# Broadcast products on VectorE, and late zero fills from SBUF, in a decode block's backward pass

## The chip, the cores and the metric

The kernel runs on one core of one Trainium2 chip. The metric is the device time of one execution in microseconds; the time before is the median of three runs. A separate view of one of these executions, the profile, records every instruction of the core's engines (PE = TensorE, DVE = VectorE, ACT = ScalarE, POOL = GpSimd, SP = SyncE) and every packet of its 16 DMA engines. L307 stands for line 307 of the kernel before, unless the kernel after is named.

## What is computed

One token passes an attention block with a sliding window over a long cache, then a gated MLP; the reference returns the output and the gradients of everything it was given.

```python
W = 4096                                   # of Sk = 32768 cached positions; 16 heads share 8 K/V heads, Dh = 256
q = layernorm(x) @ wq
p = softmax(q . k_cache[:, :, Sk-W:] / 16)
h = x + (p @ v_cache[:, :, Sk-W:]) @ wo    # D = 448
n = layernorm(h)
h2 = h + ((n @ w_gate) * (n @ w_up)) @ w_down   # F = 1792
out, vjp = jax.vjp(f, x, k_cache, v_cache, wq, wo, w_gate, w_up, w_down)
return out, *vjp(grad_out)
```

The gradients of both caches have the caches' full shape, 8 x 32768 x 256 in bf16 (134 MB each), and only the last 4096 positions of each head are not zero. So out_2 (dk) and out_3 (dv) are 235 MB of zeros and 34 MB of computed rows; the other gradients are 12 MB. The inputs that must be read are some 54 MB.

## The kernel before

**Memory.** Nearly everything lives in one tile, `arena`, [128, TOTAL] bf16, cut by hand into regions: `zeros` = columns 0 to 8191 (16 KB per partition); six 16 KB buffers A_off[0..5] behind it, which hold V of most heads and later serve as staging; M_sb (moments, f32); and a region RB reused by every stage. Columns 8192 to 16383 are A_off[0].

**Zero fills.** `fills` is a list of 103 regions of 2 MB. POOL issues them on its own queue (q0) straight from `zeros`: 42 with the full 16 KB row per partition (L135), then 13 that read only the first half of `zeros` twice (L133, packets of 8 KB), because the second half is soon needed as the weight buffer of MLP block 1. After block 1 is done, that half is zeroed again (L429) and POOL issues the remaining 48 (L430, L135). The last 18.9 MB of zeros, in head 7, are the `late_jobs`: four regions of 4 MB and one of 2 MB, issued by SP at the end of the source (L662 to L681).

**First pass** (L265 to L339). For each of 8 heads: K and V loaded by SP (L199), K transposed on PE (L255), scores, softmax, and moments, whose products are one DVE tensor_tensor of 128x2048 with a broadcast f32 operand (L307). Then wo in two halves (L322).

**Middle** (L356 to L479). Output projection (L377), layernorm, and the MLP in three blocks of 640, 512 and 640 columns. Block n's gate and down weights come through SP (L352 to L354), the up weights through ACT's queue. Blocks 0 and 2 share one buffer (in RB), block 1 uses the second half of `zeros`: its load must wait until the 42 full-width fills have read it. Per block: products with the weights (L406), diagonal expansions, and the weight-gradient reductions (L424). Then the gradients through layernorm and wo.

**Second pass** (L491 to L654). Heads in the order 2 to 7, 0, 1. For each: V transposed and dotted, a small [128, 128] factor rT, and R_sb, [128, 512], the right-hand side common to all rows. `Rbig`, [128, 8, 512], holds R_sb multiplied by each of eight masks tl_f[:, l] (L632, eight tensor_scalars per head); 32 matmuls take slices of it (L639), and their results are cast by DVE and ACT (L643 to L647) into the staging of dv (in place of V) and dk (two buffers in turn). SP stores both (L649). A staging buffer of dk is free again when the store of two heads earlier has landed.

Between heads, jobs build the weight gradients in two staging buffers `wst` (A_off[3] and A_off[4], in turn): `job_o` the rows of dwo, dh_bc times a column of oX_f, 16 tensor_scalars of 448 columns for each half; `job_d` those of dw_down, 14 of them; `job_q` and `job_qB` dwq; `expand_dg` and `job_g` dw_gate and dw_up (stores L578, L579). All use the helper scale_into (L534). At the end of the seventh head's turn DVE zeroes columns 8192 to 16383 (L654), once the store that reads them has landed.

**What sets the order.** The program text is reordered for each engine by the framework's scheduler, which keeps dependences; each engine then runs its list in order, and a DMA waits in its issuer's list. That is why SP's copies of L681, last in the source, stand among the K loads of the first pass: their source is zeros already written to DRAM, so they depend on early fills alone. The order that matters here is the one of the built programs. SP's list before, from the second pass on, is: stores of heads one to three, both parts of dwo, head four, dw_down, head five, dw_down's last part, dwq, the 2 MB late fill, dwq's last part, head six, dw_gate and dw_up, head seven, head eight.

Of the kernel before, what the change touches and what calls it, by code (L numbers as in the profile page):

```python
# [7 lines left out]
bf16 = mybir.dt.bfloat16  # L8
f32 = mybir.dt.float32
AX = mybir.AxisListType.X  # L10
ALU = mybir.AluOpType
ACT = mybir.ActivationFunctionType

D = 448
# [4 lines left out]
W = 4096  # L19
T = 32  # L20
F = 1792
NF = 14
BLOCKS = [(0, 5), (640, 4), (1152, 5)]
Sk = 32768
EPS = 1e-5
SCALE = 1.0 / 16.0
ZW = 8192
# [6 lines left out]
def kernel(  # L34
        ctx, tc, A_x, A_k_cache, A_v_cache, A_wq, A_wo, B_x, B_w_gate, B_w_up, B_w_down, grad_out,
           out_0, out_1, out_2, out_3, out_4, out_5, out_6, out_7, out_8):
    nc = tc.nc
    LD = nc.sync
# [14 lines left out]
    def ar(off, n):  # L53
        return arena[:, off:off + n]
# [4 lines left out]
    zeros = ar(0, ZW)  # L59
# [36 lines left out]
    dh2_bc = const.tile([128, D], bf16)  # L96
# [13 lines left out]
    nc.vector.memset(ones_f[:], 1.0)  # L110
    eps_t = const.tile([128, 1], f32)
    nc.vector.memset(eps_t[:], EPS)

    scratch = nc.dram_tensor("zero_row", [4 * ZW], bf16, kind="Internal").ap()
    LD.dma_start(out=scratch.rearrange("(p f) -> p f", f=ZW // 32), in_=zeros[:, 0:ZW // 32])

    def zero_rows(o, g, n0, n1, f):
        reg = o[0, g, 0:Sk - W, :].rearrange("s d -> (s d)")[n0 * 128 * ZW:n1 * 128 * ZW]
# [4 lines left out]
    for g in range(G):  # L123
        for o in (out_2, out_3):
            if g == G - 1 and o is out_3:
                continue
            reg = zero_rows(o, g, 0, 5 if g == G - 1 else NZ, ZW)
# [25 lines left out]
    tl_f = const.tile([128, 8], f32)  # L153
# [205 lines left out]
    with tc.tile_pool(name="ps_mid", bufs=3, space=bass.MemoryType.PSUM) as ps_mid, \  # L359
# [11 lines left out]
        oX_f = const.tile([128, 32], f32)  # L371
# [17 lines left out]
        hh_f = const.tile([128, NF], f32)  # L389
# [4 lines left out]
        for n in range(len(BLOCKS)):  # L394
            f0, nb, w, wgu, wd = block_views(n)
            b0 = f0 // 128
            cs = slice(b0, b0 + nb)
            for b in range(nb):
                nc.vector.tensor_tensor_reduce(out=dgb[:, 0:D], in0=wd[:, b, :], in1=dh2_bc[:], scale=1.0, scalar=0.0,
                                               op0=ALU.mult, op1=ALU.add, accum_out=d_hh[:, b0 + b:b0 + b + 1])  # L400
# [11 lines left out]
            for i in range(2):  # L412
                nc.vector.tensor_tensor(out=diag[:, 0:w].rearrange("p (m b) -> p m b", b=nb), in0=ident_f[:].unsqueeze(2).to_broadcast([128, 128, nb]),
                                        in1=dgu_f[:, i, cs].unsqueeze(1).to_broadcast([128, 128, nb]), op=ALU.mult)
# [6 lines left out]
            for c in range(4):  # L421
# [3 lines left out]
                                               op0=ALU.mult, op1=ALU.add, accum_out=dhn[0:kp, c, n:n + 1])  # L425
# [9 lines left out]
        dh_bc = const.tile([128, D], bf16)  # L435
# [18 lines left out]
        for jc in range(32):  # L454
            nc.vector.tensor_tensor_reduce(out=wo_sb[:, jc, :], in0=wo_sb[:, jc, :], in1=dh_bc[:], scale=1.0, scalar=0.0,  # L455
                                           op0=ALU.mult, op1=ALU.add, accum_out=doX_f[:, jc:jc + 1])
# [3 lines left out]
                                in1=m8_f[:].unsqueeze(2).to_broadcast([128, 8, 32]), op=ALU.mult)  # L460
# [13 lines left out]
        for dh in range(2):  # L474
# [11 lines left out]
                                scalar1=SCALE, scalar2=None, op0=ALU.mult)  # L486
# [4 lines left out]
    with tc.tile_pool(name="work2", bufs=2) as work2, tc.tile_pool(name="lnw", bufs=1) as lnw, \  # L491
# [17 lines left out]
        for c in range(3):  # L509
            nc.vector.tensor_tensor_reduce(out=wq2A[:, c, :], in0=wq2A[:, c, :], in1=dq_bc, scale=1.0, scalar=0.0,  # L510
                                           op0=ALU.mult, op1=ALU.add, accum_out=dn1[:, c:c + 1])
# [22 lines left out]
        def scale_into(out, src, col):  # L534
            nc.vector.tensor_scalar(out=out, in0=src, scalar1=col, scalar2=None, op0=ALU.mult)  # L535

        def job_o(n):
            def run():
                buf = buffer()
                for j in range(16):  # L540
                    scale_into(buf[:, j * D:(j + 1) * D], dh_bc[:], oX_f[:, 16 * n + j:16 * n + j + 1])
                LD.dma_start(out=out_5.rearrange("(p j) n -> p (j n)", j=32)[:, 16 * n * D:16 * (n + 1) * D], in_=buf[:, 0:16 * D])
            return run

        def job_d():
            buf = buffer()
            for j in range(NF):
                scale_into(buf[:, j * D:(j + 1) * D], dh2_bc[:], hh_f[:, j:j + 1])
            for f0, nb in BLOCKS:
                b0 = f0 // 128  # L550
                LD.dma_start(out=out_8[f0:f0 + 128 * nb, :].rearrange("(p b) n -> p (b n)", b=nb), in_=buf[:, b0 * D:(b0 + nb) * D])
# [49 lines left out]
        for it, g in enumerate(order):  # L601
            V_sb = kv_at(V2_off[it])
            fill_vpad(it % 2, doT_bf[:, :, 2 * g:2 * g + 2])

            def evac(q, XT, ps):
                if q % 2:
                    nc.scalar.copy(out=XT, in_=ps)  # L607
                else:
                    nc.vector.tensor_copy(out=XT, in_=ps)  # L609
            dpT_ps = dots(V_sb, VT_slot, vpad[it % 2], rows2, ps_t, "tmp", evac)  # L610

            pds = work2.tile([128, 4, 8, 4], bf16, tag="pds")
            pv = pT_all[:, g].rearrange("p (q l) h -> p q l h", q=4)
            tmp = work2.tile([128, T, 2], f32, tag="tmp2")
            nc.vector.tensor_tensor(out=tmp[:], in0=dpT_ps[:].rearrange("p q l h -> p (q l) h"),
                                    in1=delta_bc[:, 2 * g:2 * g + 2].unsqueeze(1).to_broadcast([128, T, 2]), op=ALU.subtract)
            nc.vector.tensor_copy(out=pds[:, :, :, 0:2], in_=pv)
            nc.vector.tensor_tensor(out=pds[:, :, :, 2:4], in0=tmp[:].rearrange("p (q l) h -> p q l h", q=4), in1=pv, op=ALU.mult)
            r_ps = ps_t.tile([128, 128], bf16, tag="tmp")
            nc.tensor.transpose(r_ps[:], pds[:].rearrange("p q l i -> p (q l i)"), ident_bf[:])  # L620
            rT = work2.tile([128, 128], bf16, tag="rT")
            nc.vector.tensor_copy(out=rT[:], in_=r_ps[:])
            nc.vector.tensor_copy(out=Zr, in_=Z4[:, :, :, g, :].rearrange("p w e i -> p (w e) i").unsqueeze(2).to_broadcast([128, 4, 32, 4]))
            R_ps = ps_t.tile([128, 2, 2, 128], f32, tag="tmp")
            for w in range(2):
                for dh in range(2):
                    nc.tensor.matmul(R_ps[:, w, dh, :], lhsT=Zr[:, 2 * w + dh].rearrange("p k i -> p (k i)"), rhs=ident_bf[:], start=True, stop=True)
            R_sb = work2.tile([128, 512], bf16, tag="R", bufs=1)
            nc.scalar.copy(out=R_sb[:], in_=R_ps[:].rearrange("p w e n -> p (w e n)"))
            RB_ = Rbig[it % 2]  # L630
            for l in range(8):
                nc.vector.tensor_scalar(out=RB_[:, l, :], in0=R_sb[:], scalar1=tl_f[:, l:l + 1], scalar2=None, op0=ALU.mult)  # L632
            stV, stK = V_sb, kv_at(dK_off[it % 2])
            for l in range(8):
                for qp in range(2):
                    d_ps = ps_d.tile([128, 2, 2, Dh], f32, tag="d")
                    for qi in range(2):
                        q = 2 * qp + qi
                        nc.tensor.matmul(d_ps[:, qi].rearrange("p w d -> p (w d)"), lhsT=rT[32 * q:32 * (q + 1), :], rhs=RB_[32 * q:32 * (q + 1), l, :],  # L639
                                         start=True, stop=True)  # L640
                    t = 4 * l + 2 * qp
                    if qp:
                        nc.scalar.copy(out=stV[:, t:t + 2, :], in_=d_ps[:, :, 0, :])  # L643
                        nc.scalar.copy(out=stK[:, t:t + 2, :], in_=d_ps[:, :, 1, :])  # L644
                    else:
                        nc.vector.tensor_copy(out=stV[:, t:t + 2, :], in_=d_ps[:, :, 0, :])  # L646
                        nc.vector.tensor_copy(out=stK[:, t:t + 2, :], in_=d_ps[:, :, 1, :])  # L647
            for o_ap, st_ in ((out_3, stV), (out_2, stK)):
                LD.dma_start(out=o_ap[0, g, Sk - W:, :].rearrange("(p t) d -> p t d", t=T), in_=st_)  # L649
            for job in plan[it]:  # L650
                job()
            if it == 6:

                nc.vector.memset(ar(ZW, ZW), 0.0)  # L654

        R64 = 4 * ZW
        done = out_2[0, 0, 0:Sk - W, :].rearrange("s d -> (s d)")
        other = out_3[0, 0, 0:Sk - W, :].rearrange("s d -> (s d)")

        srcs = ["same", "rows16", "rows64", "shift", "other", "scratch", "rows16_32", "same"]  # L660
        n = 0
        for o, g, n0, n1, f in late_jobs:  # L662
            reg = zero_rows(o, g, n0, n1, f)
            for i in range(reg.shape[0]):
                if f == ZW:
                    LD.dma_start(out=reg[i], in_=ar(ZW, f))
                    continue
                flat = reg[i].rearrange("p f -> (p f)")
                kind = srcs[n]
                n += 1  # L670
                w = R64 // 2 if kind == "rows16_32" else R64
                dst = flat.rearrange("(a r b) -> a r b", a=16, b=w)
                m = 2 * 128 * ZW // (16 * w)
                if kind in ("same", "scratch"):
                    src = (scratch if kind == "scratch" else done[0:w]).unsqueeze(0).unsqueeze(0).to_broadcast([16, m, w])
                elif kind in ("rows16", "rows16_32"):
                    src = done[0:16 * w].rearrange("(a r b) -> a r b", a=16, b=w).to_broadcast([16, m, w])
                else:
                    lo = {"rows64": 0, "shift": 5 * 4096 + 3 * R64, "other": 0}[kind]
                    src = (other if kind == "other" else done)[lo:lo + 16 * m * w].rearrange("(a r b) -> a r b", a=16, b=w)  # L680
                LD.dma_start(out=dst, in_=src)  # L681

# [1 line left out]
_INS = ['A_x', 'A_k_cache', 'A_v_cache', 'A_wq', 'A_wo', 'B_x', 'B_w_gate', 'B_w_up', 'B_w_down', 'grad_out']  # L684
# [26 lines left out]
```

## Time and profile before

| | |
|---|---|
| median of 3 runs | 806.97 us (805.34, 807.64, 806.97) |
| the profiled execution | 805.34 us, span 803.6 us |
| PE busy | 464.4 us, 58% |
| DVE busy | 408.8 us, 51% |
| ACT busy | 196.1 us, 24% |
| DMA moved | 334.86 MB |
| first pass ends (last L316) | 314.7 us |
| first computed store of the second pass | 522.0 us |
| last store issued by SP | 751.8 us |
| end of q0's zero fills (landed) | 785.5 us |

The profiled time contains 1.7 us around the span. "Waits" name what ended an engine's idle time. A window's row gives each engine's busy time with its number of instructions, then the granted TensorE clock, the busy share of the DMA engines and what they moved in GB/s. In a timeline row, the bracket is the idle time just before it and what ended that.

### The profile page before, as it was taken

How to read it: one execution, taken by the hardware profiler on the slowest of the kernel's cores; microseconds unless marked ns; L12 is line 12 of the kernel's file. 1: busy time of each engine (PE TensorE's matmuls, PEld its weight loads, DVE VectorE, ACT ScalarE, POOL GpSimd, SP SyncE). 2: the span in 40 equal slices, each digit the busy share in tenths (PEclk: the TensorE clock that was granted, in tenths of full speed). 3: DMA queues.
4: the chain of work that ended last, by engine and by line, in shares of the span. 5: the costliest groups of instructions: out<-in, count | busy, mean ns of one | idle time of the engine just before them, and what ended most of it. 6: DMA issues, size and time to landing. Idle time of an engine off the chain costs nothing.

```text
span 803.6 us, 7904 instructions
## 1 busy us (share of the span) xinstructions
PE 464.4 (58%) x3159; PEld 240.0 (30%) x3182; DVE 408.8 (51%) x728; ACT 196.1 (24%) x309; POOL 61.3 (8%) x112
## 2 busy tenths in 40 slices
PE   0258999999999999241232584958442700744100
PEld 0234545445455454021121471433120300311000
DVE  2115764836748575021378528848666703877200
ACT  0043124132241301000010120736342400645200
POOL 4000000000001010011011000100000000000000
PEclk9998999999999999555555695978665765767555
DMA  9999999999999999999999999999999999999995
GB/s 351 428 432 431 429 430 446 387 432 370 417 422 429 426 426 430 422 426 421 421 427 431 409 425 422 430 429 427 426 429 424 423 425 423 423 419 422 423 426 230
DMA packets 29242, 334.86 MB, mean 417 GB/s; under 512 B 2835, under 2 KB 6038, under 8 KB 7958
## 3 DMA queue, kind: packets, MB, share of 16 engines
q0 software_dynamic: 16496, 216.01, 63.7%
q1 hardware_dynamic: 11270, 116.74, 35.0%
q10 hardware_dynamic: 1440, 1.61, 0.6%
q8 instruction: 25, 0.41, 0.2%
q14 instruction: 11, 0.09, 0.0%
HBM read 70.47 MB, written 280.66 MB: 437 GB/s over the span
## 4 chain that ended last, share of the span: by engine, by line
DMA 41%; another core or an unknown queue 24%; DVE 13%; PE 9%; issue 2%; POOL 2%; ACT 1%; SPq 0%; DVEq 0%; ACTq 0%; POOLq 0%
DMA out_dram<-arena 41%; DVE arena L646 2%; DVE arena L455 2%; DVE arena L647 2%; PE dqb_ps L498 2%; PE rows_ps L258 2%; POOL out_dram L135 2%; DVE arena L510 1%; PE d_ps L639 1%; PE tr_ps L255 1%; DVE arena L535 1%; DVE arena L424 1%; PE dqb_ps L501 1%; DVE arena L632 1%
## 5 line engine op out<-in xcount | busy, mean ns | idle before, releaser
L307 DVE TENSOR_TENSOR arena<-arena,p_f 128x2048 bf16<-128x2048 bf16 x64 | 145.2, 2284 | 59.5 <-PE M_ps L312 59.5
L312 PE MATMUL M_ps<-arena 128*128 128x512 bf16 x489 | 126.4, 381 | 1.1
L255 PE MATMUL tr_ps<-ident_bf,arena 128*128 128x128 bf16 x1024 | 87.6, 236 | 22.4 <-DMA arena<-in_A_k_cache_dram 15.1
L258 PE MATMUL rows_ps<-arena,vpad 128*16 128x512 bf16 x256 | 85.4, 429 | 22.3 <-DVE arena L609 17.1
L135 POOL DMA_DIRECT2D out_dram<-arena x90 | 48.1, 536 | 608.7 <-DMA out_dram<-arena 575.9
L255 PEld LDWEIGHTS <-arena 128*128 128x128 bf16 x1024 | 65.8, 105 | 71.8 <-issue 55.6
L639 PE MATMUL d_ps<-arena,rT 32*128 32x512 bf16 x256 | 43.1, 503 | 64.5 <-DVE arena L647 44.5
L272 ACT COPY arena<-tr_ps 128x1024 bf16<-128x1024 bf16 x64 | 61.8, 1015 | 75.6 <-PE tr_ps L255 75.6
L316 PE MATMUL ok_ps<-arena 128*16 128x256 bf16 x512 | 64.5, 273 | 1.1 <-DVE arena L299 0.9
L312 PEld LDWEIGHTS <-arena 128*128 128x128 bf16 x512 | 43.3, 99 | 50.9 <-issue 15.2
L607 ACT COPY arena<-tr_ps 128x1024 bf16<-128x1024 bf16 x32 | 32.5, 1017 | 97.0 <-PE tr_ps L255 39.6
L643 ACT CAST arena<-d_ps 128x512 bf16<-128x512 f32 x64 | 37.7, 588 | 65.3 <-PE d_ps L639 65.3
L316 PEld LDWEIGHTS <-arena 128*16 128x16 bf16 x512 | 41.9, 89 | 29.8 <-issue 20.8
L646 DVE CAST arena<-d_ps 128x512 bf16<-128x512 f32 x64 | 43.9, 686 | 13.6 <-PE d_ps L639 13.3
L647 DVE CAST arena<-d_ps 128x512 bf16<-128x512 f32 x64 | 43.5, 679 | 8.7 <-DMA out_dram<-arena 8.7
L644 ACT CAST arena<-d_ps 128x512 bf16<-128x512 f32 x64 | 38.2, 596 | 9.3 <-DMA out_dram<-arena 9.3
L639 PEld LDWEIGHTS <-rT 32*128 32x128 bf16 x256 | 11.2, 95 | 90.2 <-issue 51.8
L258 PEld LDWEIGHTS <-vpad 128*16 128x16 bf16 x256 | 18.9, 90 | 56.1 <-issue 48.1
L406 PE MATMUL gu_ps<-X_b,arena 128*128 128x1 bf16 x112 | 10.0, 187 | 28.9 <-DMA arena<-in_B_w_gate_dram 28.8
L287 ACT ACTIVATE e_f<-cols_ps,nbias 128x32 f32<-128x32 f32 x16 | 4.5, 285 | 85.7 <-DVE nbias L283 85.7
L260 DVE COPY arena<-rows_ps 16x512 f32<-16x512 f32 x16 | 10.8, 676 | 28.3 <-PE rows_ps L258 28.3
L510 DVE CUSTOM_DVE_ANT_0 arena<-arena 128x4096 bf16<-128x4096 bf16 x3 | 13.1, 4423 | 23.5 <-ACT arena L503 23.5
(198 smaller groups left out, 381.6 us busy)
## 6 DMA issues: line engine op xcount, KB each, us to landing
out_dram<-arena POOLq DMA_DIRECT2D x103, 2048.0 KB, 54.9
out_dram<-arena SPq DMA_DIRECT2D x18, 2048.0 KB, 29.6
arena<-in_A_v_cache_dram SPq DMA_DIRECT2D x10, 2048.0 KB, 52.0
arena<-in_A_k_cache_dram SPq DMA_DIRECT2D x8, 2048.0 KB, 33.3
arena<-in_A_wq_dram SPq DMA_DIRECT2D x2, 3072.0 KB, 20.6
arena<-in_A_wo_dram SPq DMA_DIRECT2D x2, 1792.0 KB, 18.6
out_dram<-arena SPq DMA_DIRECT2D x2, 1792.0 KB, 33.1
out_dram<-arena SPq DMA_DIRECT2D x2, 1344.0 KB, 48.5
```

The source lines that it names most:

```text
L135: ZQ.dma_start(out=reg, in_=zeros)
L255: nc.tensor.transpose(tr_ps[:, dh, i, :], X_sb[:, 4 * q + i, dh * 128:(dh + 1) * 128], ident_bf[:])
L258: nc.tensor.matmul(rows_ps[:], lhsT=pad[:, dh, 16 * q:16 * q + 16], rhs=XT[:, dh].rearrange("p t k -> p (t k)"), start=(q == 0 and dh == 0 ...
L272: sT_ps = dots(kv_at(K_off[g]), KT_slot, vpad[g % 2], rows1, ps_c, "cols", lambda q, XT, ps: nc.scalar.copy(out=XT, in_=ps))
L307: nc.vector.tensor_tensor(out=pK, in0=K_sb[:, 4 * c:4 * c + 4, :].unsqueeze(2).to_broadcast([128, 4, 2, Dh]), in1=p_f[:, c::8, :].unsqueez ...
L312: nc.tensor.matmul(M_ps[:, vh, :], lhsT=V_sb[:, t, vh * 128:(vh + 1) * 128], rhs=pK[:, i, :, :].rearrange("p h d -> p (h d)"), start=(t == ...
L316: nc.tensor.matmul(ok_ps[:, k, :], lhsT=ppad[g % 2][:, 8 * (t % 4) + t // 4, :], rhs=X_sb[:, t, :], start=(g == 0 and k == 0 and t == 0), ...
L639: nc.tensor.matmul(d_ps[:, qi].rearrange("p w d -> p (w d)"), lhsT=rT[32 * q:32 * (q + 1), :], rhs=RB_[32 * q:32 * (q + 1), l, :], start=T ...
L643: nc.scalar.copy(out=stV[:, t:t + 2, :], in_=d_ps[:, :, 0, :])
L644: nc.scalar.copy(out=stK[:, t:t + 2, :], in_=d_ps[:, :, 1, :])
L646: nc.vector.tensor_copy(out=stV[:, t:t + 2, :], in_=d_ps[:, :, 0, :])
L647: nc.vector.tensor_copy(out=stK[:, t:t + 2, :], in_=d_ps[:, :, 1, :])
```

## The change

Three edits of the computing code and one of the fills:

1. The eight masked copies of R_sb per head become one tensor_tensor of 128x4096, R_sb broadcast over the masks times tl_f broadcast over the columns (f32).
2. Each half of dwo's rows becomes one tensor_tensor of 128x7168 and
3. dw_down's rows one of 128x6272, in the same manner.
4. The four late 4 MB regions are no longer copied from zeroed DRAM in several patterns of source, but stored from columns 0 to 16383 of `arena`, 32 KB per partition, after both halves are zero; the 2 MB one is stored from columns 8192 to 16383 as before. The 64 KB DRAM scratch row and its store are gone.

```diff
-    scratch = nc.dram_tensor("zero_row", [4 * ZW], bf16, kind="Internal").ap()
-    LD.dma_start(out=scratch.rearrange("(p f) -> p f", f=ZW // 32), in_=zeros[:, 0:ZW // 32])
...
-                for j in range(16):
-                    scale_into(buf[:, j * D:(j + 1) * D], dh_bc[:], oX_f[:, 16 * n + j:16 * n + j + 1])
+                nc.vector.tensor_tensor(out=buf[:, 0:16 * D].rearrange("p (j n) -> p j n", n=D), in0=dh_bc[:].unsqueeze(1).to_broadcast([128, 16, D]),
+                                        in1=oX_f[:, 16 * n:16 * n + 16].unsqueeze(2).to_broadcast([128, 16, D]), op=ALU.mult)
...
-            for j in range(NF):
-                scale_into(buf[:, j * D:(j + 1) * D], dh2_bc[:], hh_f[:, j:j + 1])
+            nc.vector.tensor_tensor(out=buf[:, 0:NF * D].rearrange("p (j n) -> p j n", n=D), in0=dh2_bc[:].unsqueeze(1).to_broadcast([128, NF, D]),
+                                    in1=hh_f[:].unsqueeze(2).to_broadcast([128, NF, D]), op=ALU.mult)
...
-            for l in range(8):
-                nc.vector.tensor_scalar(out=RB_[:, l, :], in0=R_sb[:], scalar1=tl_f[:, l:l + 1], scalar2=None, op0=ALU.mult)
+            nc.vector.tensor_tensor(out=RB_, in0=R_sb[:].unsqueeze(1).to_broadcast([128, 8, 512]),
+                                    in1=tl_f[:].unsqueeze(2).to_broadcast([128, 8, 512]), op=ALU.mult)
...
-        R64 = 4 * ZW
-        done = out_2[0, 0, 0:Sk - W, :].rearrange("s d -> (s d)")
-        other = out_3[0, 0, 0:Sk - W, :].rearrange("s d -> (s d)")
-
-        srcs = ["same", "rows16", "rows64", "shift", "other", "scratch", "rows16_32", "same"]
-        n = 0
         for o, g, n0, n1, f in late_jobs:
             reg = zero_rows(o, g, n0, n1, f)
             for i in range(reg.shape[0]):
-                if f == ZW:
-                    LD.dma_start(out=reg[i], in_=ar(ZW, f))
-                    continue
...
-                if kind in ("same", "scratch"):
-                    src = (scratch if kind == "scratch" else done[0:w]).unsqueeze(0).unsqueeze(0).to_broadcast([16, m, w])
-                elif kind in ("rows16", "rows16_32"):
-                    src = done[0:16 * w].rearrange("(a r b) -> a r b", a=16, b=w).to_broadcast([16, m, w])
-                else:
-                    lo = {"rows64": 0, "shift": 5 * 4096 + 3 * R64, "other": 0}[kind]
-                    src = (other if kind == "other" else done)[lo:lo + 16 * m * w].rearrange("(a r b) -> a r b", a=16, b=w)
-                LD.dma_start(out=dst, in_=src)
+                LD.dma_start(out=reg[i], in_=ar(2 * ZW - f, f))
```

Of the eight names in `srcs` the four regions take the first four: the same 64 KB row again and again, sixteen rows repeated, and twice 64 distinct rows.

In the built programs, PE's and ACT's lists are the same up to the second pass, DVE's up to the first product of edit 1, and POOL's throughout. SP's list loses the scratch store and the four copies; from the second pass on it is (lines of the kernel after): heads one and two, first part of dwo (L539), head three, all of dw_down (L548), second part of dwo, first part of dwq (L590), head four, dwq (L585), head five, dwq's last part (L592), a 4 MB fill (L656), head six, dw_gate and dw_up (L575, L576), head seven, a 4 MB fill, head eight, two 4 MB fills and the 2 MB fill. DVE's product of edit 1 is L628 there, its zeroing of columns 8192 to 16383 is L651 and stands among the sixth head's casts.

More of the change, by code (lines that the diff above doesn't have):

```diff
@@ L664 @@
             for i in range(reg.shape[0]):
-                if f == ZW:
-                    LD.dma_start(out=reg[i], in_=ar(ZW, f))
-                    continue
[L668 to L673, printed above, removed]
-                if kind in ("same", "scratch"):
-                    src = (scratch if kind == "scratch" else done[0:w]).unsqueeze(0).unsqueeze(0).to_broadcast([16, m, w])
-                elif kind in ("rows16", "rows16_32"):
-                    src = done[0:16 * w].rearrange("(a r b) -> a r b", a=16, b=w).to_broadcast([16, m, w])
-                else:
-                    lo = {"rows64": 0, "shift": 5 * 4096 + 3 * R64, "other": 0}[kind]
-                    src = (other if kind == "other" else done)[lo:lo + 16 * m * w].rearrange("(a r b) -> a r b", a=16, b=w)
-                LD.dma_start(out=dst, in_=src)
+                LD.dma_start(out=reg[i], in_=ar(2 * ZW - f, f))
 _INS = ['A_x', 'A_k_cache', 'A_v_cache', 'A_wq', 'A_wo', 'B_x', 'B_w_gate', 'B_w_up', 'B_w_down', 'grad_out']
```

## The prediction

> **What bounds the kernel now.** I read the page's DMA rows and queues first, then stretches of the span, then the engines' timelines around the places where a queue waits.
>
> ```profile
> DMA  9999999999999999999999999999999999999995
> DMA packets 29242, 334.86 MB, mean 417 GB/s; under 512 B 2835, under 2 KB 6038, under 8 KB 7958
> q0 software_dynamic: 16496, 216.01, 63.7%
> q1 hardware_dynamic: 11270, 116.74, 35.0%
> HBM read 70.47 MB, written 280.66 MB: 437 GB/s over the span
> ```
>
> The two big queues, q0 (POOL's zero fills) and q1 (everything SP issues), fill 98.7% of the time of 16 DMA engines. Every slice but the last is full. The bound is DMA engine time; compute matters only where it leaves the engines without a packet.
>
> ```profile
> 140.00:220.00 80.00, 78.18 (x502) 38.09 (x509) 51.96 (x48) 20.63 (x34) 2.65 (x5) 1.00 1.01 408
> 220.00:260.00 40.00, 39.65 (x271) 20.74 (x272) 26.49 (x26) 10.50 (x16) 3.19 (x6) 1.00 0.98 415
> 260.00:300.00 40.00, 39.65 (x253) 19.40 (x256) 25.86 (x21) 9.43 (x14) 3.71 (x7) 1.00 1.01 427
> 780.00:804.00 24.00, 0.00 (x0) 0.00 (x0) 0.00 (x0) 0.00 (x0) 0.00 (x0) 0.50 0.60 255
> ```
>
> These rows end in granted clock, DMA share and GB/s. The four DRAM-to-DRAM copies are issued at 98.5, 130.8, 131.5 and 196.0 us (L681) and land by 225: while they run the engines are as busy, but move 408 to 415 GB/s instead of 427. The last row is the tail: by the landing records the last store lands on the fastest engine at 790.0 and on the slowest at 802.5. That slowest engine has been late in q0 all along (8 us behind the fastest at 411), never without work, and sets the end.
>
> ```profile
> 384.46 0.67 POOL L133 DMA_DIRECT2D out_dram<-arena  x1 [4.46 <-DMA out_dram<-arena]
> 389.83 0.66 POOL L133 DMA_DIRECT2D out_dram<-arena  x1 [4.70 <-DMA out_dram<-arena]
> 411.40 2.13 POOL L135 DMA_DIRECT2D out_dram<-arena  x4 [20.91 <-DVE arena L429]
> 336.61 5.46 PE L377 MATMUL ao_ps<-arena,oX_bf 128*1 128x448 bf16 x16 [15.56 <-DMA arena<-in_A_wo_dram]
> 377.11 2.42 PE L406 MATMUL gu_ps<-X_b,arena 64*128 64x1 bf16 x29 [1.27 <-DMA arena<-in_B_w_gate_dram]
> ```
>
> POOL runs out of permitted fills at 389.83 and may go on only after the memset of L429, which closes MLP block 1. The fills already queued last until 426.2 (mean engine) and 431.7 (slowest) by the landing records, so today nothing runs dry.
>
> **The change, part by part.**
>
> *Copies out, fills from SBUF in.* Four copies of 4.19 MB leave the early q1; four SBUF-to-DRAM fills of the same bytes enter its late part, two of them behind the very last stores. Bytes written are equal, the 64 KB scratch store aside. Price by the stretches: (427-408) x 80 + (427-415) x 40 = 2.0 MB not moved, less (435-427) x 40 = 0.3 MB gained in 100 to 140, so 1.7 MB / 427 GB/s = 3.9 us. Checked by packets: a 64 KB copy packet takes 2.656 us against 4 x 0.615 for the same bytes from SBUF; 16 per engine make 3.2 us, the rest being slower fill packets beside them. Term: **-3.9** (bounds -3.2 and -5.2, the latter without the gain of 100 to 140). A 32 KB row from SBUF is not in the trace; 8 KB take 0.309 and 16 KB 0.611 us, so I give it the same rate.
>
> The Trainium skill ("DMA: Bandwidth & Descriptors", Specifications) gives one core about 358 GB/s of HBM. By that limit the 351.1 MB read and written would need 981 us, and sparing 16.8 MB of reads would gain 47; the row above shows 437 GB/s, so that limit did not bind here.
>
> *Where q0 gets that time.* Copies cost each engine 16 x 2.656 = 42.5 us before POOL's pause. Without them, and with their side effect gone (about 1.3 us), the queued fills end at 426.2 - 43.8 = 382.4, on the slowest engine 387.9. So POOL's resumption must come earlier too. Does it?
> - SP's load of block 1 (second L352) now waits for the 42 full fills, until 360.8. At 309.5 us q0 had moved 72.5 MB by the packet records; 16.8 + 1.8 more make 91.1, above the 88.1 MB of the 42. They land at about 300 to 305, before that load's turn at 315.
> - From 300 on q0 therefore consists of the half-width fills, whose packets take 0.309 us and not 0.615. Queues take turns packet by packet, so loads pass faster. Per engine: w_down block 0, 8 x (0.173 + 0.309) = 3.9 instead of 6.3; block 1, 3.6 instead of 6.0; second half of wo, 8 x (0.535 + 0.309) = 6.8 instead of 9.2; gate block 0, 24 x 0.36 = 8.6 instead of 16.0 (15.3 seen). Starting at 308.8 as now, wo lands at 327.3 (now 335.4) and gate block 0 at 335.9 (now 350.7).
> - Gate block 1 follows directly: 24 x 0.349 + 1.4, 345.7. The up half waits on ACT behind the layernorm's root, about 335, then three queues: 24 x 0.40 plus some 3 us of latency, 348 to 349. PE reaches block 1 near 349 instead of 377.1.
> - From there to POOL took 411.4 - 377.1 = 34.3 us; again, 383.3. From issue to first packet POOL took 5.0 us at the start (5.1 to 10.1), so packets flow at about 388.4.
>
> The mean engine idles 6 us, the slowest, which sets the end, 0.5. I take **+1.2**. Bounds: 0, and, if the loads gain nothing and POOL stays at 411.4, 416.4 - 387.9 = 28.5.
>
> *Masked right-hand sides.* Added per head: one product of 128x4096, bf16 times an f32 broadcast, instead of eight tensor_scalars.
>
> ```profile
> 682.54 2.19 DVE L632 TENSOR_SCALAR arena<-R_sb,tl_f 128x512 bf16<-128x512 bf16 x8
> L307 DVE TENSOR_TENSOR arena<-arena,p_f 128x2048 bf16<-128x2048 bf16 x64 | 145.2, 2284 | 59.5 <-PE M_ps L312 59.5
> ```
>
> L307 is the same form at half the width; from the chained starts of L307 (13.44 us for six) 2.24 each, so 4.42 per head against 2.19: +2.2, eight times, 17.8. The first matmul also waits for all 4.4 us rather than one eighth of 2.2.
>
> *dwo and dw_down rows.* Two times 7168 elements: 7.7 us each against 16 x 0.245 = 3.9; 6272 elements: 6.7 against 3.4. +10.9, DVE +28.7 in all. If the narrow bf16 products had kept their rate, it would be zero: that is the lower bound.
>
> The Trainium skill's "VectorE: DVE Perf Modes" (The perf-mode tier table) allows tensor_tensor on bf16 two elements a cycle and one with fp32, tensor_scalar four. With the first, a head's product would be about 2.3 us and the change free; L307 shows the second.
>
> What hides the 28.7: in the chain of waits, DVE's second pass stands on landing stores for 15.58 + 16.41 + 33.12 + 47.43 + 35.33 = 147.9 us between 522 and 737, and DMA is full meanwhile. What it costs without cover: behind the last stores SP has 4.2 MB of stores and 10.5 MB of fills, 14.7 / 0.427 = 34.4 us, and the slowest engine ends some 8 us after the mean; with an end near 801 less 1.5 of closing, the last store may be issued at 755 for nothing. Today it is at 751.8, and the pass starts 28 us earlier: 724 with everything hidden. All on the path: + 28.7, and + 4.2 MB / 0.2135 = 19.6 us because the first late fill stands ahead of the sixth head's stores in SP's order, whose landing frees the eighth head's staging: 772, so 17 too late. I take 0 (the halfway value, 748, is below 755); ends 0 and +17.
>
> On the queues: SP's order also moves dw_down before the second dwo part and the first dwq part before the fourth head. In order, SP then holds those stores for DVE's product; q0 fills the engines meanwhile. POOL's instructions do not change.
>
> **Sum.** 803.6 - 3.9 + 1.2 + 0 = 800.9 span; the run with this profile was 805.34, 1.7 more, so 802.6. The median of the three runs lies 1.6 above that run: 806.97 - 2.7 = **804.3**.
>
> **Rivals.**
> 1. *POOL's pause runs the engines dry* (slower). One mechanism: the memset of L429 does not come forward with q0. For it: margin was only 14.8 us on the mean engine, and the lead is 43.8. Against: the waits that held it (360.8) fall with the same lead. It decides from 5 us of idle on the slowest engine; with the loads of block 1 alone advanced (14 us), POOL at 397.4, packets at 402.4, idle 14.5: 806.97 - 3.9 + 14.5 = 817.6. Chance 0.20.
> 2. *DVE becomes the bound* (slower): last store after 755, a fair middle between 748 and 772 being 760 to 765; +8: 812. Against: 147.9 us of landing waits. Chance 0.13.
> 3. *HBM traffic is the bound*: 16.8 MB / 437 GB/s = 38 off, 769. Against: the engines were no less busy without copies. Chance 0.03.
> 4. *Nothing visible*: idle of 2.5 to 5 us eats the copies' gain, 806. It differs from the forecast in that one term. Chance 0.20.
>
> Forecast 0.44, its own range 800.5 to 807 with rival 4. About 0.3% (2.4 us) is what a measurement of this kernel can tell from no change: faster is below 804.5. The forecast's point lies barely inside, so of its 0.44 about 0.03 falls to the same, which leaves 0.41 and 0.03 for rival 3: faster 0.44. Same: 0.20 + 0.03 + 0.03 from rivals 1 and 2 at their small ends = 0.26. Slower 0.30. Range: bottom 799 (-5.2, no idle, 2 less for the runs' spread); top 817, rival 1's price.
>
> **What would show it.** GB/s near 427 through 100 to 260; POOL's full fills resuming near 383, SP's second load of block 1 near 316; L628 rows near 4.4 us; q0 gone by 740 to 770; DMA share at 1.0 from 390 to 785 and no slice below. A share well under 1.0 between 380 and 410 is rival 1; one between the last stores, rival 2. A rate unlike 0.61 us per 16 KB in the late fills would make the copy term wrong.

## The result, and the profile after

The kernel after takes 799.8 us (median of four runs, 799.6 to 800.0); the kernel before, run beside it on the same chip, 807.3 (805.3 to 808.0). The ratio is 0.9911, with a 95% interval of 0.9893 to 0.9929: 7.5 us or 0.9% faster, where 2.7 us were forecast. The profiled execution took 799.98 us, its span is 798.2. All runs of the kernel before, those beside the experiments too, lay in two groups, 805.3 to 807.0 and 807.4 to 809.5, the four of the kernel after in one; differences below 0.3% are therefore read from the spans and the packets, not from medians.

The page's DMA rows of the kernel after:

```profile
DMA  9999999999999999999999999999999999999995
DMA packets 29354, 334.80 MB, mean 419 GB/s; under 512 B 2819, under 2 KB 5894, under 8 KB 7814
q0 software_dynamic: 16496, 216.01, 64.0%
q1 hardware_dynamic: 11382, 116.68, 34.8%
HBM read 53.69 MB, written 280.59 MB: 419 GB/s over the span
```

No slice but the last is below full, as before: DMA engine time is still the bound. The copies' 16.8 MB of reads are gone, and the same bytes went out at 419 instead of 417 GB/s.

The stretches shown for the kernel before, in the kernel after (granted clock, DMA share and GB/s end each row):

```profile
140.00:220.00 80.00, 79.25 (x520) 39.71 (x525) 54.94 (x53) 20.57 (x34) 7.44 (x14) 1.00 1.01 430
220.00:260.00 40.00, 39.53 (x282) 20.32 (x283) 20.55 (x20) 13.28 (x18) 3.72 (x7) 1.00 1.01 423
380.00:390.00 10.00, 5.11 (x25) 2.63 (x25) 6.97 (x19) 2.52 (x5) 4.22 (x8) 0.50 1.01 423
760.00:780.00 20.00, 0.00 (x0) 0.00 (x0) 0.00 (x0) 0.00 (x0) 0.00 (x0) 0.50 1.03 440
780.00:798.00 18.00, 0.00 (x0) 0.00 (x0) 0.00 (x0) 0.00 (x0) 0.00 (x0) 0.50 0.56 238
```

Where the copies ran, 408 and 415 GB/s became 430 and 423. These rows count a packet whole in the stretch where it starts. With each packet split at the stretches' edges, the kernel before moved 404 GB/s between 140 and 220 and 428 between 220 and 260, so the whole dent lies in the first of the two. The third row is the place where POOL's pause could have run the engines dry: they are full. The fourth is the late fills: 440 GB/s at a share of 1.03, 431 with the packets split. Nothing is paid back there.

The timelines of POOL, PE and SP at the prediction's points:

```profile
343.68 0.66 POOL L130 DMA_DIRECT2D out_dram<-arena  x1 [5.51 <-DMA out_dram<-arena]
380.73 3.68 POOL L132 DMA_DIRECT2D out_dram<-arena  x7 [36.39 <-DVE arena L426]
324.44 5.74 PE L374 MATMUL ao_ps<-arena,oX_bf 128*1 128x448 bf16 x16 [7.81 <-DMA arena<-in_A_wo_dram]
348.13 1.15 PE L403 MATMUL gu_ps<-X_b,arena 64*128 64x1 bf16 x13 [1.02 <-DMA arena<-in_B_w_up_dram]
735.38 1.73 SPq L646 DMA_DIRECT2D out_dram<-arena  x2
740.01 4.82 SPq L656 DMA_DIRECT2D out_dram<-arena  x3
```

POOL runs out of permitted fills at 343.7 instead of 389.8 and resumes at 380.7 instead of 411.4. PE has wo at 324.4 and starts on block 1 at 348.1. The last head's stores are issued at 735.4 and 736.0, and three fills follow.

The costliest group among the changed products:

```profile
L628 DVE TENSOR_TENSOR arena<-R_sb,tl_f 128x4096 bf16<-128x4096 bf16 x8 | 35.4, 4419 | 0.7 <-ACT R_sb L626 0.7
```

The product takes 4.419 us, as predicted from half its width. DVE's busy time rose from 408.8 to 437.0.

### The profile page after: what moved, and what is told of

Its sections match the earlier page's. It is cut to its first block, busy times and chain, and to the rows that moved or that the text cites. A ratio compares the mean times of both kernels' runs of the same rounds, so it can differ in the third digit from the quotient of the medians.

```text
span 798.2 us, 7807 instructions
## 1 busy us (share of the span) xinstructions
PE 480.3 (60%) x3159; PEld 245.3 (31%) x3182; DVE 437.0 (55%) x629; ACT 195.9 (25%) x309; POOL 61.4 (8%) x112
## 4 chain that ended last, share of the span: by engine, by line
DMA 47%; another core or an unknown queue 15%; DVE 14%; PE 9%; issue 3%; ACT 2%; POOL 1%; SPq 0%; DVEq 0%; ACTq 0%; POOLq 0%
DMA out_dram<-arena 47%; DVE arena L628 2%; DVE arena L452 2%; PE dqb_ps L495 2%; DVE arena L643 2%; PE rows_ps L255 2%; PE d_ps L636 2%; PE tr_ps L252 1%; DVE arena L644 1%; DVE arena L507 1%; POOL out_dram L132 1%; DVE arena L421 1%; PE dqb_ps L498 1%; DVE arena L537 1%
## 5 line engine op out<-in xcount | busy, mean ns | idle before, releaser
L636 PE MATMUL d_ps<-arena,rT 32*128 32x512 bf16 x256 | 46.9, 531 | 111.0 <-DVE arena L644 63.8
L252 PE MATMUL tr_ps<-ident_bf,arena 128*128 128x128 bf16 x1024 | 91.7, 241 | 18.8 <-ACT arena L604 11.3
L255 PE MATMUL rows_ps<-arena,vpad 128*16 128x512 bf16 x256 | 90.4, 451 | 20.6 <-DVE arena L606 14.6
L252 PEld LDWEIGHTS <-arena 128*128 128x128 bf16 x1024 | 68.4, 108 | 70.7 <-issue 62.7
L309 PEld LDWEIGHTS <-arena 128*128 128x128 bf16 x512 | 43.3, 99 | 50.9 <-issue 15.2
L628 DVE TENSOR_TENSOR arena<-R_sb,tl_f 128x4096 bf16<-128x4096 bf16 x8 | 35.4, 4419 | 0.7 <-ACT R_sb L626 0.7
```

The lines of the kernel that those rows point to most:

```text
L252: nc.tensor.transpose(tr_ps[:, dh, i, :], X_sb[:, 4 * q + i, dh * 128:(dh + 1) * 128], ident_bf[:])
L255: nc.tensor.matmul(rows_ps[:], lhsT=pad[:, dh, 16 * q:16 * q + 16], rhs=XT[:, dh].rearrange("p t k -> p (t k)"), start=(q == 0 and dh == 0 ...
L309: nc.tensor.matmul(M_ps[:, vh, :], lhsT=V_sb[:, t, vh * 128:(vh + 1) * 128], rhs=pK[:, i, :, :].rearrange("p h d -> p (h d)"), start=(t == ...
L628: nc.vector.tensor_tensor(out=RB_, in0=R_sb[:].unsqueeze(1).to_broadcast([128, 8, 512]), in1=tl_f[:].unsqueeze(2).to_broadcast([128, 8, 51 ...
```

## The experiments

Packet times and landings below are summed from the trace's packet and landing records. All are in us. "All packets" is the sum of packet times, a mean over the 16 engines; "zeros" means the time of one 64 KB of the last 16.8 MB of zeros, however it is cut; the spread is between the first and the last engine to land the last store.

| kernel | median | all packets | zeros | spread | last landing |
|---|---|---|---|---|---|
| before | 807.3 | 798.8 | 2.656 | 12.5 | 802.5 |
| after | 799.8 | 794.9 | 2.444 | 8.4 | 797.1 |
| fills only | 800.1 | 795.4 | 2.449 | 7.7 | 797.2 |
| products only | 805.9 | 800.6 | 2.702 | 12.0 | 802.6 |
| 59 fills ahead of the pause | 799.95 | 795.1 | 2.444 | 9.6 | 797.0 |
| product twice | 799.7 | 794.6 | 2.455 | 3.9 | 796.6 |
| early copies, distinct rows | 808.1 | 800.0 | 2.692 | 12.5 | 803.7 |
| before without scratch | 806.8 | 800.1 | 2.695 | 11.9 | 802.6 |
| early copies, one 16 KB row | 801.5 | 796.8 | 2.46 | 7.8 | 798.6 |
| late copies, 64 KB | 812.8 | 806.4 | 3.117 | 6.2 | 811.3 |
| late copies, 16 KB row | 808.3 | 802.1 | 2.79 | 6.7 | 806.0 |
| after with scratch | 802.1 | 796.2 | 2.444 | 5.1 | 798.2 |

Four kernels make the same early copies in 64 KB packets (before, products only, distinct rows, without scratch). Their sums still differ by 1.8 us, from 798.8 to 800.6, so a difference of that size between two single profiles is not read as an effect.

**Fills only.** The kernel before with the fills of the kernel after and without the scratch row; all products stay narrow.

```diff
-    scratch = nc.dram_tensor("zero_row", [4 * ZW], bf16, kind="Internal").ap()
-    LD.dma_start(out=scratch.rearrange("(p f) -> p f", f=ZW // 32), in_=zeros[:, 0:ZW // 32])
...
-                LD.dma_start(out=dst, in_=src)
+                LD.dma_start(out=reg[i], in_=ar(2 * ZW - f, f))
```

> The kernel before with the late fills stored from SBUF and without the scratch row; the narrow products stay. Theory (DMA time is the bound and the fills are the whole effect): the time of the kernel after, 799.8 us, within 1.5; sum of DMA packet times per engine 794.9 us as in the profile after (before 798.8). Rival (the products cost time that the fills' gain hides): 2 to 8 us faster than the kernel after, 792 to 798. Rival (the products help): slower than the kernel after, 802 or more.

Measured: 800.1 us (799.6 to 802.7), ratio 0.9914 (0.9896 to 0.9932). The fills are the whole effect.

**Products only.** The kernel before with the three products; the copies stay.

> The kernel before with the three broadcast products alone; the DRAM-to-DRAM copies and the scratch row stay. Theory: DVE busy rises by 28 us to 437 and the time stays at that of the kernel before, 807.3 within 1.5, its sum of DMA packet times at 798.8 per engine. Rival (products on the path): 2 to 15 us slower.

Measured: 805.9 us (805.4 to 807.2), ratio 0.9981 (0.9971 to 0.9990), with the copies at their old place:

```profile
140.00:220.00 80.00, 78.20 (x507) 37.88 (x508) 51.81 (x48) 20.42 (x34) 2.65 (x5) 1.00 1.01 405
220.00:260.00 40.00, 39.81 (x274) 20.82 (x273) 26.64 (x26) 10.50 (x16) 3.19 (x6) 1.00 0.97 415
```

The dent belongs to the copies. The span is 803.7 against 803.6: the products cost nothing and bring nothing there. That the median is 0.2% lower is not explained; it lies within what the kernel before's own runs differ by.

**Fewer fills ahead of the pause.** The kernel after with four fills less permitted before POOL's pause.

```diff
-HALF0, HALF1 = 42, 55
+HALF0, HALF1 = 42, 51
```

> The kernel after with 51 instead of 55 zero fills ahead of POOL's pause, the four others behind it. Theory (in the kernel after the queued fills last just to the end of the pause: landed at 383.3 on the mean engine, next packets at about 386): 8.4 MB or 19.6 us less is queued, so the engines stand idle 13 to 18 us near 370 to 385 and the time is 811 to 817. Rival (the pause does not bound, the end comes from the second pass): 799.8 within 1.

Measured: 814.2 us (813.8 to 814.5), ratio 1.0082 (1.0069 to 1.0096). Its stretches around the pause, and the instruction that ends it:

```profile
340.00:360.00 20.00, 7.43 (x45) 3.31 (x43) 9.41 (x22) 1.51 (x4) 0.00 (x0) 0.50 1.01 422
360.00:380.00 20.00, 6.21 (x48) 4.04 (x49) 10.09 (x23) 1.29 (x4) 1.71 (x4) 0.50 0.22 82
...
378.29 4.20 POOL L132 DMA_DIRECT2D out_dram<-arena  x8 [63.47 <-DVE arena L426]
```

The share of 0.22 is what engines without packets look like: POOL waits 63 us for the memset, and 16.0 us of engine time are lost by the packet records. The time grew by 14.4 us, nearly the whole idle: rival 1's mechanism is real, and the kernel after has almost no margin against it.

**More fills ahead of the pause.** The same with 59.

> The kernel after with 59 fills ahead of the pause. Theory: the fast engines no longer wait at the pause, but the slowest never did, so the time stays at 799.8 within 1 and the spread between fastest and slowest engine at the last landing goes from 8.4 us back toward the 12.5 of the kernel before. Rival (the 1 to 5 us of idle on the mean engine count): 1 to 4 us faster, spread unchanged.

Measured: 799.95 us (799.8 to 800.1), ratio 0.9907 (0.9892 to 0.9923), no idle at all. Nothing is left to gain there. The spread was expected to go back to 12.5 and is 9.6, so the pause is not what evens the engines out in the kernel after.

**DVE's cover, once and twice.** The kernel after with each head's masked product computed two and three times, 35 and 71 us more of DVE (the diff is of the first).

```diff
-            nc.vector.tensor_tensor(out=RB_, in0=R_sb[:].unsqueeze(1).to_broadcast([128, 8, 512]),
+            for _ in range(2):
+                nc.vector.tensor_tensor(out=RB_, in0=R_sb[:].unsqueeze(1).to_broadcast([128, 8, 512]),
```

> The kernel after with each head's masked product issued twice into the same buffer: DVE busy +35 us, 472. Theory (the second pass runs ahead of the DMA queues and has some 12 us to spare behind the last head's stores, which go out at 735 against a limit near 750, besides its waits for landing stores): the last head's stores go out at 740 to 755 and the time is 799.8 to 803. Rival (every DVE microsecond of the second pass is on the path): last stores at 770, time 820 or more.

> The same with three issues: DVE busy +71 us, 508. Theory: the cover is used up; the last head's stores go out at 755 to 785 and the time is 804 to 825, with the DMA share under 1.0 somewhere between 730 and 785. Rival (the cover is wider: DVE is never near the bound): 800 to 802 and no stretch under 1.0.

Measured: 799.7 us (799.5 to 800.1) and 821.5 (818.9 to 822.5), ratios 0.9913 (0.9897 to 0.9929) and 1.0177 (1.0155 to 1.0200). With two products, the tail shows:

```profile
740.00:760.00 20.00, 3.58 (x25) 1.07 (x25) 15.07 (x14) 5.19 (x10) 0.00 (x0) 0.53 1.00 426
760.00:780.00 20.00, 2.14 (x16) 0.33 (x12) 5.15 (x8) 4.29 (x8) 0.00 (x0) 0.50 0.87 369
...
741.64 1.25 SPq L657 DMA_DIRECT2D out_dram<-arena  x1
767.07 0.93 SPq L647 DMA_DIRECT2D out_dram<-arena  x2
768.05 2.47 SPq L657 DMA_DIRECT2D out_dram<-arena  x2
```

The last stores go out at 767, 31 us later than in the kernel after, and the engines do run dry (0.87; 2.5 us idle between 760 and 785 by the packet records), yet the time is the same, at stores later than expected (740 to 755). By the landing records 15 engines finish at 792.7 to 792.9 and one at 796.6. So the gap cost time that the 15 had to spare; that the last one had a backlog throughout follows from its landing and was not seen by itself. The edit also changed SP's order: here a 4 MB fill (741.64) goes out ahead of the last head's stores, and only two fills follow (768.05), where the kernel after has three. From these stores on SP then has 10.5 MB to move, instead of the 14.7 from which the limit of 755 was worked out; by the same sum that is 9.8 us less work and a limit of 765. With three products:

```profile
700.00:720.00 20.00, 12.66 (x76) 5.04 (x75) 17.39 (x23) 8.27 (x15) 0.00 (x0) 0.59 0.57 240
720.00:740.00 20.00, 13.32 (x78) 5.99 (x77) 17.83 (x31) 10.00 (x14) 0.00 (x0) 0.74 0.86 363
760.00:780.00 20.00, 5.40 (x40) 2.02 (x36) 17.51 (x19) 7.75 (x14) 0.00 (x0) 0.59 0.46 193
...
799.80 0.93 SPq L647 DMA_DIRECT2D out_dram<-arena  x2
```

Now DVE is busy 17 to 18 of 20 us and the engines wait for stores at 0.57, 0.86 and 0.46: rival 2, at some point between 35 and 71 us of added DVE work, with SP's order changed again (one fill of 2 MB behind the last stores).

**Copies cut into rows of 16 KB.** The kernel before with all four copies reading distinct rows of 16 KB.

```diff
-        srcs = ["same", "rows16", "rows64", "shift", "other", "scratch", "rows16_32", "same"]
+        srcs = ["rows64"] * 4
-                w = R64 // 2 if kind == "rows16_32" else R64
+                w = R64 // 4
```

> The kernel before with its four DRAM copies cut into rows of 16 KB instead of 64 KB, all from distinct rows of one 4 MB source. Theory A (the DRAM source is what is slow): packets of 16 KB between 0.65 and 0.68 us against 0.615 from SBUF, and the time stays at that of the kernel before, 807.5 within 2. Theory B (the 64 KB packet is what is slow or uneven): packets at 0.62, spread between engines at the last landing near 8 us instead of 12.5, time 800 to 803.

Measured: 808.1 us (805.5 to 808.8), ratio 1.0008 (0.9994 to 1.0022). The test was not made: neighbouring rows were joined, and the trace again has 256 packets of 65,536 B, of 2.692 us. It shows only that distinct rows cost what the mixed patterns do. The kernel before's own four copies say the same: with one row repeated, sixteen rows and twice 64 distinct rows they took 2.60 to 2.74 us per packet, so down to one row of 64 KB the choice of source rows is not what costs.

**No scratch row.** The kernel before without the scratch row and its store.

> The kernel before without the 64 KB scratch row, which none of the four copies reads. Its store has 8 packets of 512 B per engine, each a turn behind a 16 KB fill packet (8 x 0.62 = 5 us), ahead of the first K load. Theory: the first pass ends some 5 us earlier (309 instead of 314.7), and the time does not move: 807.5 within 1.5. Rival (part of the change's gain came from this): 802 to 805.

Measured: 806.8 us (805.5 to 808.7), ratio 1.0006 (0.9993 to 1.0018). The first pass ends at 310.0 instead of 314.7, and the time does not move.

**Copies from one 16 KB row.** The kernel before with all four copies repeating one row, which can't be joined.

```diff
-        srcs = ["same", "rows16", "rows64", "shift", "other", "scratch", "rows16_32", "same"]
+        srcs = ["same"] * 4
-                w = R64 // 2 if kind == "rows16_32" else R64
+                w = R64 // 4
```

> The kernel before, its four copies left in the early part of SP's list, but each reads one 16 KB row of zeroed DRAM again and again, so that neighbouring rows can't be merged into 64 KB packets. Theory A (a DRAM source is dear in itself): the copies' 16 KB packets take 0.65 to 0.69 us, four of them as much as the 2.66 us of a 64 KB one, and the time stays with before, 806 to 808.5, last landing spread over some 12 us. Theory B (the packet of 64 KB is dear): 0.61 to 0.63 us for 16 KB, the copies cost each engine 39.5 us and not 42.5, and the time is 801 to 804.

Measured: 801.5 us (801.2 to 805.1), ratio 0.9947 (0.9928 to 0.9965). The same DRAM-to-DRAM bytes, still in the early part of SP's list (two copies at 99.7 to 101, two at 131 to 138):

```profile
140.00:220.00 80.00, 44.76 (x275) 21.71 (x280) 28.39 (x26) 11.35 (x16) 4.25 (x8) 0.77 1.01 429
220.00:260.00 40.00, 39.65 (x256) 19.52 (x258) 27.09 (x30) 10.08 (x18) 2.66 (x5) 1.00 1.01 429
```

The dent is gone (429 GB/s), the 16 KB packets take 0.614 us, the price from SBUF, the fills beside them 0.615 instead of 0.644, and the spread fell to 7.8. So here reading from DRAM was not what cost; copying in 64 KB packets was. Why such a packet is dearer no run shows. PE is busy only 45 of 80 us: its K loads wait behind more packets, and the first pass ends at 351.7. That costs little, since the engines stay full but for 0.9 us at POOL's pause, which ends at 421.8.

**The copies late.** The kernel before with a source that POOL fills only after its pause, which puts the copies where the kernel after has its fills; first in 64 KB packets, as in this diff, then from one 16 KB row, with `w = R64 // 4` besides.

```diff
-        done = out_2[0, 0, 0:Sk - W, :].rearrange("s d -> (s d)")
+        done = fills[75].rearrange("p f -> (p f)")
-        srcs = ["same", "rows16", "rows64", "shift", "other", "scratch", "rows16_32", "same"]
+        srcs = ["same"] * 4
```

> The kernel before with its narrow products, its scratch store and its four copies in packets of 64 KB, but with a source that POOL fills only after its pause: SP's list then holds the copies where the kernel after holds its four late fills. Theory A (a copy has its price wherever it runs): the sum of packet times stays within 1 us of before's 798.8, some 3 us more than in the run with the fills alone (795.4), and the time is 803 to 808. Theory C (the price comes from the place, beside the reads of the first pass): packets of 2.45 to 2.55 us, and 799.5 to 802. If the unevenness of the engines is made by the copies whenever they run, the last landing spreads over 12 us again; if it is made only by copies among the early loads, over some 8 us.

> The kernel with the copies late, but in packets of 16 KB from one repeated row, so that they run with hardly any other packets beside them. Theory B (the packet of 64 KB is dear): 0.61 to 0.63 us for 16 KB as in the early copies, the sum of packet times 796 to 798, and 800 to 806. Theory D (a copy is dear where most engines copy at once; at half the packets in the early part it cost nothing): 0.74 to 0.84 us where no fills of POOL are left, and 807 to 813.

Measured: 812.8 us (812.3 to 814.2), ratio 1.0079 (1.0064 to 1.0093), and 808.3 (807.9 to 809.4), ratio 1.0011 (0.9997 to 1.0025). The 64 KB kernel early, at the pause, and at the end:

```profile
140.00:220.00 80.00, 79.14 (x513) 38.75 (x519) 52.42 (x49) 21.43 (x34) 6.91 (x13) 1.00 1.01 429
380.00:390.00 10.00, 2.02 (x5) 0.57 (x6) 9.48 (x24) 0.47 (x1) 3.41 (x7) 0.50 0.56 233
780.00:800.00 20.00, 0.00 (x0) 0.00 (x0) 0.00 (x0) 0.00 (x0) 0.00 (x0) 0.50 1.00 312
...
386.59 4.20 POOL L135 DMA_DIRECT2D out_dram<-arena  x8 [43.62 <-DVE arena L429]
```

The first kernel went as neither of its theories had it: late copies are dearer than early ones, 3.117 us per 64 KB packet, 3.10 for those started between 760 and 780 and 3.35 between 780 and 800, where almost nothing else was left, and 312 GB/s with every engine full. Early reads are thus not what makes a copy dear. The 16 KB packets, 0.614 us early, came to 0.697 on average late, less than a quarter of 3.117 and more than the 0.61 that packet size alone would give. In the second kernel the time fell into what theory D expected, with an average price between the two theories. The average hides two prices. Taken in the order of their starts, the packets of the first two copies, beside POOL's fills, took 0.62 and 0.63 us; those of the last two, after POOL's last fill packet at 750.9, took 0.77, within the 0.74 to 0.84 of theory D. (The order is not exact, as the engines are some us apart.) Of the 64 KB packets, the first copy's, beside POOL's fills, took 2.88. So size and company both count: late, four packets of 16 KB cost 2.5 us beside fills and 3.1 without, one of 64 KB 2.88 and 3.35. The second surprise is the pause: POOL resumes at 386.6, not 380.7, and 4.7 us of idle appear (4.4 in the other kernel). These two kernels differ from the kernel after up to there only in the scratch store.

**The kernel after, with the scratch store.** That store put back, nothing else.

```diff
+    scratch = nc.dram_tensor("zero_row", [4 * ZW], bf16, kind="Internal").ap()
+    LD.dma_start(out=scratch.rearrange("(p f) -> p f", f=ZW // 32), in_=zeros[:, 0:ZW // 32])
```

> The kernel after, with the 64 KB scratch store put back ahead of the first K load, where the kernel before has it. If that store's 5 us of delay in the first pass decide the pause (as the two kernels with late copies suggest, where POOL went on at 386), POOL goes on at 385.5 to 387, the engines lack packets for 3.5 to 5 us between 380 and 390, and the time is 802.5 to 805. If the scratch only moves compute, as it did in the kernel before, POOL still goes on by 382 and the time stays at 799.5 to 800.5.

Measured: 802.1 us (800.7 to 802.7), ratio to before 0.9926 (0.9908 to 0.9943):

```profile
380.00:390.00 10.00, 2.89 (x14) 1.44 (x15) 9.48 (x24) 1.01 (x1) 4.21 (x8) 0.50 0.69 278
...
385.13 4.21 POOL L135 DMA_DIRECT2D out_dram<-arena  x8 [41.58 <-DVE arena L429]
```

POOL is 4.4 us later (expected 385.5 to 387, so 0.4 earlier than that) and the share in this stretch is 0.69 instead of 1.01; 3.4 us are idle by the packet records. The time, 0.4 us below what was expected, is 2.3 us above the median of the kernel after, and no run of the one reaches the other's; but the two were not run side by side, their ratios to before overlap, and by the spans the difference is 1.1 (799.3 against 798.2). Part of the idle is not paid: the spread shrank to 5.1, because the late engine, with packets left, kept working. A 64 KB store that is worth nothing in the kernel before decides here whether the engines run dry at the pause; what that costs, 1.1 us by the spans and 2.3 by the medians, is less than the idle.

No version was faster than the kernel after beyond the scatter of the runs; with 59 fills ahead of the pause, or each product twice, it is the same.

## Why the prediction was right, and what it missed

- *The bound, and the sign.* Right. DMA engine time bounds both kernels, the fills carry the whole gain, the products none. The size was not: 7.5 us against 2.7, so that 799.8 lies below the forecast's own range of 800.5 to 807 and just above the bottom of the whole range, 799.
- *Copies out, fills in, -3.9.* The end is set by the engine that lands last, and its last landing came forward by 5.4, from 802.5 to 797.1. That is beyond the forecast's -5.2. It is firm: the four kernels with early 64 KB copies land at 802.5 to 803.7, the kernel after and three near it (fills only, 59 fills, product twice) at 796.6 to 797.2. On the mean engine the packet times fell from 798.8 to 794.9, just the 3.9, but that the two agree so well is partly luck: the other three kernels with these copies have 800.0 to 800.6. The price of a 32 KB row from SBUF, taken from 16 KB rows as 1.23, measured 1.222. The slowdown read in 220 to 260 belongs to 140 to 220, as said above; the two errors of the window rows nearly cancel in the sum. The step charged the change to an average engine and kept the lag of the slowest, "some 8 us after the mean", as a constant. It is 7.6 us before and 6.1 after, but 6.3 with the products alone, so how the 5.4 divide between all engines and the last one is not settled. The spread is clearer: 11.9 to 12.5 in the four kernels with early 64 KB copies, 7.7 to 9.6 in the kernel after, with the fills only, with 59 fills, and with early copies in 16 KB packets. Early 64 KB packets go with uneven engines. Why one engine lags at all was not settled.
- *The idle at the pause, +1.2.* Measured 0.2. The end of the queued fills was right (382.4 and 387.9 predicted on the mean and the slowest engine, 383.3 and 387.7 measured). The resumption came earlier, by two errors. One: POOL's first packet after the pause came 1.2 us after its issue (380.73, 381.9), and not the 5.0 taken from its very first issue of the kernel. Two: the scratch store, set aside as 64 KB, stood ahead of the first K load on SP, and without it the first pass ends at 308.6 instead of 314.7; with it back, at 313.6, and POOL is 4.4 us later. So the walk through the loads, which began at 308.8, should have begun at 302.7. That its stages still came out near (wo 327.3 predicted, 324.4 measured; block 1 on PE 349, 348.1; POOL 383.3, 380.7) is luck: from its start the walk was 3 to 5 us too short, which hid most of the 6.1.
- *DVE +28.7 at nothing.* Measured +28.2 and nothing. The last stores went out at 735.4, between the 724 and 748 worked out, with some 20 us to spare before 755. Whether 755 was the right limit stays open: the run with stores at 767 had 4.2 MB less to move from there on, so that by the prediction's own sum its limit was 765, which it passed by 2 us at no cost.
- *From span to median.* The sum added to the time after the 1.6 us by which before's median lay above its profiled run. Those three runs differed by 2.3 us; the four of the kernel after differ by 0.4, and their median lies 0.2 below the profiled run.
- *The size, put together.* Forecast 804.3, measured 799.8: 1.5 for the copies and fills (5.4 at the end instead of 3.9), 1.2 for the idle that did not come (its price was worked out on the slowest engine too), 1.6 for the carry to the median, and 0.2 between after's profiled run and its median make the 4.5.
- *The rivals.* Rival 1 did not happen, but fewer fills ahead of the pause or the old scratch store bring its idle time in (16.0 and 3.4 us). Rival 2 lies beyond 35 us more of DVE work. Rival 3, which asked for 769, did not happen, and one run speaks against it more directly: between 780 and 800 of the kernel with late copies, 312 GB/s are moved and nearly all of it is copies (95 packets of 64 KB started there are 6.23 of 6.24 MB), so 624 GB/s were read and written together, far above the 437 of the whole span before and the 358 that the Trainium skill states ("DMA: Bandwidth & Descriptors", Specifications).

## What to carry to other kernels

When DMA engine time is the bound, price a change by packet times, and then ask what it does to the engine that lands last, since only that one sets the end; slack of the others hides gaps and costs. When work on a full queue is brought forward, follow everything that gates its refill back to its start: a small store that was free as long as the refill had margin can cost time when the margin is gone. Zeros that are in SBUF anyway were better stored from there than copied within DRAM, unless the copies were cut small and ran beside other traffic. And an edit that only lengthens one instruction can change the order of another engine's list: read the built order before calling the run a test of a limit.

## What the runs showed of the hardware

- A DRAM-to-DRAM copy in 64 KB packets took 2.66 us each beside other queues early in the kernel, 2.88 beside POOL's fills late, and 3.35 with almost nothing else running (780 to 800), and slowed the 16 KB fill packets beside it from 0.614 to 0.644 us; in packets of 16 KB from one repeated row it took 0.614 early, 0.62 to 0.63 late beside fills and 0.77 after the fills had ended.
- Contiguous rows of 16 KB came out as packets of 65,536 B; one repeated row did not.
- A store of 8 packets of 512 B per engine, issued just ahead of a load on the same queue, moved the end of the first pass by 5 us (314.7 to 310.0 in the kernel before without it, 308.6 to 313.6 in the kernel after with it).
- After a pause, POOL's queue had its first packets 1.1 to 1.2 us after the issue (380.73 to 381.9, 385.13 to 386.2, 386.59 to 387.7); after its first issue of the kernel before, 5.0 us (5.1 to 10.1).
